# A compile-time scheduler that plans transfers on a shared server, tile turns apart from data, and the first rows in one buffer

## Chip, cores, metric

The kernel runs on one core of a Trainium2 chip. The metric is the device time of one execution in microseconds (us), the median of several runs. The engines are TensorE (PE in the profile, with its weight loader PEld), VectorE (DVE), ScalarE (ACT), GpSimd (POOL), and SyncE (SP), which issues all DMAs of this kernel.

## What is computed

Attention with normalised queries and keys (batch 8, 12 heads, 448 rows, head size 64), followed by two matrix products with `h * cos(h)` between them, all in float32:

```python
def rmsnorm(x, g):
    rms = np.sqrt(np.mean(x * x, axis=-1, keepdims=True) + 1e-06)
    return x / rms * g
q_n, k_n = (rmsnorm(q, g_q), rmsnorm(k, g_k))
scores = 1.0 / np.sqrt(64) * np.matmul(q_n, k_n.transpose(0, 1, 3, 2))
attn = np.exp(scores - np.max(scores, axis=-1, keepdims=True))
attn = attn / (np.sum(attn, axis=-1, keepdims=True) + 1e-09)
x = np.matmul(attn, v).transpose(0, 2, 1, 3).reshape(3584, 768)
h = x @ w_in                      # 768 x 2048
out = (h * np.cos(h)) @ w_out     # 2048 x 768
```

## The kernel before

**The work.** Two heads make a pair; there are 48 pairs `u`, six for each of the 8 batches `b`. Pairs 0 to 5 (`plain`) run in full float32. From pair 6 on each operand is split into a high part and a rest (`hi`, `lo`; `khi`, `kl`; `qhi`, `ql`) in a shorter float format, and products are sums over the parts.

For each pair: `st_load` brings the rows of q and k as `sd`; `st_square` (ACT) and `st_reduce` (DVE) make their sums of squares `r`; `st_pow` (POOL) makes the reciprocal roots; `st_store` and `rk_load` carry those of k through DRAM (`rk_d`) and back, spread over the partitions as `rkb`; `k_norm` and `q_scale` (POOL) apply them; `m_place`, `d_place` and `e_place` are DMAs that lay out the split operands for the score products. For the first two pairs (`turned`, `u < NKT`) k is normalised in rows (`kn_load`, `kn_square`, `kn_reduce`, `kn_pow`, `kn_norm`), turned by TensorE (`kn_turn`) and copied out as `km` (`kn_copy`, which needs the weight vector that `g_load` and `g_fold` make).

Then come seven score tiles per pair (`score_plain` or `score`, PE), `rowmin` (DVE), `expo` (ACT), the turning of the seven results (`transp`, PE, into the two banks `PT`), their copies (`pt_copy`, or `pt_high` on ACT and `pt_low` on DVE), and the product with v (`av`, PE).

The first product of the second layer, `ffn1`, of batch `b` fills TensorE between the attention steps of the next batch; its result `h` goes to DRAM (`h_out` on ACT into one of two `he` buffers, then `h_store`). Weights arrive as 64-bit numbers and are decoded to float32 in five steps (`w_load`, `w_decode` for w_in; `v_fetch`, `v_decode` for w_out), four on DVE and one on ACT. The second layer's product is a Strassen scheme: sums of quarters of w_out (`v_sum`, `v_split`) go back to DRAM (`wo_d`).

After the attention a second stage begins (at about 952 us): `ffn1_block` for the last batch, 16 blocks on 8 PSUM banks, block `fc` in bank `fc % 8`; meanwhile `h` is loaded back (`gl_load`), `h * cos(h)` is made and split, and `w_place` loads the weights of the second product from `wo_d` into slots that the w_in weights leave one by one. The rest is `ffn2`, in products P1 to P7, three banks each.

**The order.** Every step is handed to a class `Plan` with an engine, a cost in us, a due time, the keys it reads and writes, and, for a DMA, a time `land` from issue to data. `Plan.order()` then runs a list schedule at compile time: each engine takes, of the steps that can run, the one with the earliest due time. What comes out is only an order: each engine's instructions stand in its queue in this order, and the hardware's semaphores do the waiting. So a step that waits holds up all that stand behind it on its engine. `RING` says how many buffers a tile has; a tile's first user depends on all users of the tile that had the buffer before.

Of the kernel before, what the change touches and what calls it, by code (L numbers as in the profile page):

```python
# [10 lines left out]
F32 = mybir.dt.float32  # L11
# [12 lines left out]
class Plan:  # L24
# [3 lines left out]

    SIGNAL = {"PE": 0.25, "ACT": 0.19, "DVE": 0.16, "POOL": 0.15, "SP": 0.16}
    LEAD = 0.3

# [9 lines left out]
    def add(self, eng, cost, due, fn, *args, r=(), w=(), land=0.0, start=0.0, lead=None):  # L43
# [17 lines left out]
        self.parts.append((eng, cost, due, fn, args, deps, land))  # L61
# [3 lines left out]
    def order(self):  # L65
        parts = self.parts
        for (name, inst), users in self.users.items():
# [6 lines left out]
        left = [len(p[5]) for p in parts]  # L74
        ready = list(self.start)
        for n, p in enumerate(parts):
            for d in p[5]:
                after[d].append(n)
# [6 lines left out]
        seq = []  # L85
        self.busy = dict.fromkeys(free, 0.0)
        while True:
# [17 lines left out]
            cost, fn, args, land = (parts[n][i] for i in (1, 3, 4, 6))  # L105
            end = free[e] = t + cost
            self.busy[e] += cost
            seq.append((t, n, fn, args))
            for m in after[n]:
# [13 lines left out]
def tile_attention_moe(  # L123
# [163 lines left out]
    for t in qlow:  # L287
        nc.vector.tensor_scalar(
            t[64:128], ident[64:128, 0:1].broadcast_to([64, 384]), 0.0, 0.0, op0=ALU.mult, op1=ALU.add
        )  # L290
# [8 lines left out]

    def st_load(u):  # L300
        n = st_cols(u)
        nc.sync.dma_start(tl(u, "sd", [128, 14, D], F32)[:, :n], sd_in[u, :, :n])

    def st_square(u):
        sdf = pair[u]["sd"][:, : st_cols(u)].rearrange("p t d -> p (t d)")
        nc.scalar.activation(sdf, sdf, AF.Square)

    def st_reduce(u):
        n = st_cols(u)
        nc.vector.tensor_reduce(tl(u, "r", [128, 14], F32)[:, :n], pair[u].pop("sd")[:, :n], axis=AX.X, op=ALU.add)  # L310
# [393 lines left out]
    ISS, LAND = 0.45, 5.0  # L704
# [11 lines left out]
    add(SP, ISS, 0.0, g_load, w=[("g", 0)], land=LAND)  # L716
    add(DVE, 0.16, 10.0, g_fold, r=[("g", 0)], w=[("gsc", 0)])

    def weights(fc):
# [3 lines left out]
        add(SP, ISS, d - 30.0, w_load, fc, w=[w if f64 else f], land=8.0, start=begin)  # L723
# [11 lines left out]
    def weights2(c):  # L735
# [4 lines left out]
        for k in range(4):  # L740
            st, f, e = ("wf", NFC + 4 * c + k), qk[k], d + 0.1 * span * k
            if f64:
                add(SP, ISS, e - 20.0, v_fetch, c, k, w=[st], land=LAND, start=e - 30.0)
# [3 lines left out]
            else:  # L747
                add(SP, ISS, e - 20.0, v_fetch, c, k, w=[f], land=LAND, start=e - 30.0)
# [6 lines left out]
        for n, (name, src, _) in enumerate(SPLITS):  # L755
# [10 lines left out]
            add(SP, ISS, e + 5.0, v_store, c, p, r=[o], land=LAND)  # L766

    def prepare(u):
        D0 = base(u)
        sd, r, kd, khi, qd, qhi = ([(n, u)] for n in ("sd", "r", "kd", "khi", "qd", "qhi"))  # L770
        turned, plain = u < NKT, u < NP
        if turned:
            kn, rn, kb = [("qd" if u == 0 else "ql", u)], [("rn", u)], [("pt", 0, n) for n in ((0,) if u == 0 else (1, 2))]
            add(SP, ISS, D0 - 60, kn_load, u, w=kn, land=3.5)
# [6 lines left out]
        else:  # L781
            add(SP, ISS, D0 - 36, k_load, u, w=kd, land=LAND)
        add(SP, ISS, D0 - 45, st_load, u, w=sd, land=4.0 if turned else 6.5)
        add(SP, ISS, D0 - 44 if turned else D0 - 30, q_load, u, w=[("qp", u)] if plain else qd, land=3.5 if turned else LAND)
# [3 lines left out]
        if not turned:  # L788
            add(SP, ISS, D0 - 30, st_store, u, r=r, w=[("rkd", u)], land=LAND)
            add(SP, 2 * ISS, D0 - 26, rk_load, u, r=[("rkd", u)], w=[("rkb", u)], land=6.5)  # L790
# [313 lines left out]
```

## Time and profile before

| | |
|---|---|
| median of 3 runs | 1425.78 us (1423.07 to 1426.09) |
| profiled execution | 1433.95 us, of which the span from first to last instruction is 1432.0 us |
| mean granted TensorE clock | 0.993 |
| busy: PE, PEld | 1386.1 us (97%), 1196.7 us (84%) |
| busy: DVE, ACT, POOL | 1078.4 us (75%), 916.6 us (64%), 654.3 us (46%) |
| DMA | 301.88 MB, mean 211 GB/s |
| chain that ended last | PE 73%, DVE 13%, DMA 5%, ACT 3% |

The prediction's rows come from one profiled execution, and its times count from the span's start. A line L469 is line 469 of the kernel before. In a group or a timeline row, `S<-S,r` names the tile written and the tiles read; square brackets give the idle time of the engine before the instruction and what ended it.

### The profile page before, as it was taken

The page shows a single profiled execution, that of the slowest core. Times are in us where ns is not written, and L with a number is a line of the kernel's source. Part 1 is how long each engine was busy: PE and PEld are TensorE (multiplying, and loading weights), DVE is VectorE, ACT ScalarE, POOL GpSimd, SP SyncE. Part 2 cuts the span into 40 slices and gives each one's busy share as a digit, 9 for nine tenths or more (in the row PEclk, how much of TensorE's full clock was granted, in tenths as well). Part 3 has the DMA queues.
Part 4 walks back from the last instruction along what each step waited for, and adds up shares of the span by engine and source line. Part 5 has one row for each costly group of instructions (what it writes and reads, how often), then busy time and mean ns, then how long its engine had stood idle before and what let it go on. Part 6 is the DMA issues. An engine that isn't in the chain of part 4 may idle for free.

```text
span 1432.0 us, 22475 instructions
## 1 busy us (share of the span) xinstructions
PE 1386.1 (97%) x7118; PEld 1196.7 (84%) x7118; DVE 1078.4 (75%) x1864; ACT 916.6 (64%) x1868; POOL 654.3 (46%) x634
## 2 busy tenths in 40 slices
PE   5999999999999999999998999999999999999999
PEld 2346888889888888889897999989999999999998
DVE  6796999787878787786968665527669979879843
ACT  4676787777776866777776776646447457356331
POOL 5579988866866766686685674120000000000000
PEclk8999999999999999999999999999999999999999
DMA  6588767787778686867868765259768568468434
GB/s 217 174 241 244 207 166 212 219 243 230 232 221 243 204 249 202 241 197 227 241 203 249 203 204 143 73 173 341 235 197 296 162 212 298 144 222 289 125 108 146
DMA packets 169478, 301.88 MB, mean 211 GB/s; under 512 B 28512, under 2 KB 123568, under 8 KB 169360
## 3 DMA queue, kind: packets, MB, share of 16 engines
q1 hardware_dynamic: 169360, 300.45, 68.8%
q8 instruction: 56, 0.92, 0.3%
q14 instruction: 62, 0.51, 0.1%
HBM read 193.59 MB, written 62.73 MB: 179 GB/s over the span
## 4 chain that ended last, share of the span: by engine, by line
PE 73%; DVE 13%; DMA 5%; ACT 3%; issue 2%; SPq 1%; POOL 1%; POOLq 0%; DVEq 0%; ACTq 0%
PE y L683 10%; PE y L681 10%; PE y L682 10%; PE PT L510 7%; PE ph L614 6%; PE ph L615 6%; PE ph L616 6%; PE O L546 6%; PE S L465 6%; DVE S L469 3%; DVE lo L529 2%; PE y L615 1%; PE y L616 1%; PE y L614 1%; DMA rawo<-w_out 1%
## 5 line engine op out<-in xcount | busy, mean ns | idle before, releaser
L469 DVE TENSOR_SCALAR_CACHE_REDUCE S<-S,r 128x448 f32<-128x448 f32 x336 | 225.2, 685 | 71.5 <-PE S L465 65.4
L614 PE MATMUL ph<-xs,wi 128*128 128x448 f32 x672 | 256.5, 382 | 4.8 <-ACT he L626 4.7
L477 ACT ACTIVATE P<-S,sm 128x448 f32<-128x448 f32 x336 | 213.1, 636 | 70.8 <-DVE S L469 66.8
L681 PE MATMUL y<-g,wo 128*128 128x448 f32 x672 | 247.3, 368 | 0.0
L682 PE MATMUL y<-g,wo 128*128 128x448 f32 x672 | 247.3, 368 | 0.0
L683 PE MATMUL y<-g,wo 128*128 128x448 f32 x672 | 247.3, 368 | 0.0
L615 PE MATMUL ph<-xs,wi 128*128 128x448 f32 x672 | 246.2, 366 | 0.0
L616 PE MATMUL ph<-xs,wi 128*128 128x448 f32 x672 | 245.8, 366 | 0.0
L661 ACT CAST g<-gq 128x896 fp32r<-128x896 f32 x112 | 105.6, 943 | 184.1 <-PE y L683 161.7
L522 ACT CAST hi<-PT 128x512 fp32r<-128x512 f32 (+1 forms) x336 | 167.3, 533 | 70.5 <-PE PT L510 65.6
L510 PEld LDWEIGHTS PT<-ident,P 128*128 128x128 f32 (+1 forms) x1344 | 158.7, 134 | 49.3 <-issue 25.9
L529 DVE TENSOR_TENSOR lo<-PT,hi 128x512 fp32r<-128x512 f32 x252 | 149.8, 615 | 63.2 <-ACT hi L522 55.5
L510 PE MATMUL PT<-ident,P 128*128 128x128 f32 (+1 forms) x1344 | 195.7, 276 | 1.3 <-ACT P L477 1.3
L659 DVE TENSOR_TENSOR g<-gq,g 128x896 fp32r<-128x896 f32 x112 | 122.2, 1091 | 89.5 <-ACT g L661 89.0
L614 PEld LDWEIGHTS ph<-xs,wi 128*128 128x128 f32 x672 | 126.7, 189 | 17.5 <-ACT he L626 8.1
L683 PEld LDWEIGHTS y<-g,wo 128*128 128x128 f32 x672 | 126.1, 188 | 12.9
L682 PEld LDWEIGHTS y<-g,wo 128*128 128x128 f32 x672 | 126.1, 188 | 12.7
L681 PEld LDWEIGHTS y<-g,wo 128*128 128x128 f32 x672 | 126.1, 188 | 12.6
L616 PEld LDWEIGHTS ph<-xs,wi 128*128 128x128 f32 x672 | 126.5, 188 | 11.3
L615 PEld LDWEIGHTS ph<-xs,wi 128*128 128x128 f32 x672 | 126.9, 189 | 9.0
L316 POOL TENSOR_TENSOR r<-r,nhalf 128x14 f32<-128x14 f32 (+1 forms) x48 | 124.1, 2585 | 4.0
L546 PE MATMUL O<-hi,vs 128*128 128x448 f32 x336 | 121.3, 377 | 4.3 <-ACT hi L522 3.0
(102 smaller groups left out, 2602.9 us busy)
## 6 DMA issues: line engine op xcount, KB each, us to landing
wo<-wo_d SPq DMA_DIRECT2D x152, 384.0 KB
h_d<-he SPq DMA_DIRECT2D x128, 224.0 KB
gq<-h_d SPq DMA_DIRECT2D x64, 448.0 KB
wo_d<-ao SPq DMA_DIRECT2D x56, 384.0 KB
sd<-sd SPq DMA_DIRECT2D x46, 448.0 KB
D<-qhi SPq DMA_DIRECT2D x168, 96.0 KB
raw<-w_in SPq DMA_DIRECT2D x16, 768.0 KB
rawo<-w_out SPq DMA_DIRECT2D x32, 384.0 KB
```

The lines of the kernel that those rows point to most:

```text
L469: nc.vector.tensor_scalar(d["S", t][:, :S], d["S", t][:, :S], d["r"][:, t : t + 1], None, op0=ALU.mult, op1=ALU.min, accum_out=d["sm"][:, ...
L477: nc.scalar.activation(tl(u, f"P{t}", [128, S], F32, "P"), d.pop(("S", t))[:, :S], AF.Exp, bias=sm[:, 1, t : t + 1], scale=-1.0, accum_out ...
L510: nc.tensor.transpose(pt[part][:n, i * 128 : i * 128 + 128], src, ident)
L522: nc.scalar.copy(hi[:n], pt[part][:n, : WIDE[part]])
L529: nc.vector.tensor_tensor(lo, src, hi.bitcast(F32), ALU.subtract)
L546: nc.tensor.matmul(O, st, d[what, kc][:, HEADS[hh]], start=(kc + n == 0), stop=(kc == 3))
L614: nc.tensor.matmul(ph[:, :S], whi, x2[:, 0, :], start=(cc == 0), stop=False)
L615: nc.tensor.matmul(ph[:, :S], whi, x2[:, 1, :], start=False, stop=False)
L616: nc.tensor.matmul(ph[:, :S], wlo, x2[:, 0, :], start=False, stop=(cc == NCC - 1))
L681: nc.tensor.matmul(y, whi, hi[:, e], start=first and e == 0, stop=False, **more)
L682: nc.tensor.matmul(y, whi, lo[:, e], start=False, stop=False, **more)
L683: nc.tensor.matmul(y, wlo, hi[:, e], start=False, stop=last and e == NG - 1, **more)
```

## The change

No computation is added or taken away, and the cost and due time of every compute step stay. What differs:

1. **Transfers in the plan.** A DMA step now gives its size (`kb`) instead of a landing time. The plan keeps one clock `moved` for all transfers, which advances by size over 270 KB per us; a transfer is done at the later of its issue plus a flight by kind (5 to 7 us; 2.4 us for issues in the first 12 us) and `moved` plus 1.2 us.
2. **Tile turns apart from data.** Two dependencies that only keep tiles in their turn (the first user of one instance behind the first user of the one before; every user behind its tile's first user) no longer carry the landing and signal times, only the order.
3. **First rows.** The rows of pairs 0 and 1 share one `sd` buffer, half each, so that the second load needs no release.
4. **Early loads.** `k_load`, `st_load`, `q_load`, `v_plain` and `v_load` get start times tied to their pair; the three clears of the `E` tiles become steps of the plan (due 24 us) instead of standing at the head of DVE's queue.

Since every transfer's time is another in the plan, the order changes along the whole kernel, on all engines but TensorE in the second stage, whose order is the same.

The diff, cut to its core (the other lines replace `land=` by `kb=` with the transfer's size):

```diff
+    RATE = 270.0
+    FLIGHT = {
+        "st_load": 7.0, "m_place": 6.5, "d_place": 6.5, "e_place": 6.5, "v_load": 5.5, "v_fetch": 7.0, "w_load": 7.0,
+        "v_store": 6.0, "rk_load": 6.0, "rs_load": 6.0,
+    }
+    FLY = 5.0
...
         for (name, inst), users in self.users.items():
             parts[users[0]][5].update(self.users.get((name, inst - self.rings[name]), ()))
-            parts[users[0]][5].update(self.users.get((name, inst - 1), ())[:1])
             parts[users[0]][5].discard(users[0])
+            behind[users[0]].update(self.users.get((name, inst - 1), ())[:1])
             for n in users[1:]:
-                parts[n][5].add(users[0])
+                behind[n].add(users[0])
...
-            end = free[e] = t + cost
+            end = free[e] = done = t + cost
+            if kb:
+                moved = max(moved, end) + kb / self.RATE
+                fly = self.FLIGHT.get(fn.__name__, self.FLY) if t > 12.0 else 2.4
+                done = max(end + fly, moved + 1.2)
...
-                same = parts[m][0] == e and not land
-                gap = 0.0 if same else land + self.SIGNAL[e] + self.lead[m]
-                ready[m] = max(ready[m], end + gap)
+                if not full:
+                    ready[m] = max(ready[m], end)
+                elif parts[m][0] == e and not kb:
+                    ready[m] = max(ready[m], end)
+                else:
+                    ready[m] = max(ready[m], done + self.SIGNAL[e] + self.lead[m])
...
+    def sd_tile(u):
+        return pair[0]["sd"][:, 7 * u : 7 * u + 7] if u < NKT else pair[u]["sd"]
...
+        sd = [("sd", max(u, NKT - 1), u)]
...
-        add(SP, ISS, D0 - 45, st_load, u, w=sd, land=4.0 if turned else 6.5)
+        add(SP, ISS, D0 - 45, st_load, u, w=sd, kb=224.0 if turned else 448.0, start=0.0 if u < NP else D0 - 60)
...
+    for i in range(RING["E"]):
+        add(DVE, 0.31, 24.0 + i, e_clear, i, w=[("E0", i)], start=20.0)
```

What it moves, at three places. First, the head of SP's queue. Rows name the source line, the operation, the tile written and read, its shape, and how often the row repeats. Before, from the second `kn` on (`sd_113` and `sd_143` are the rows of pairs 0 and 1, `raw` a weight of w_in):

```order
L322 DMA kn_111<-kn 112x512
L302 DMA sd_113<-sd 128x448
L380 DMA q_98<-qT 128x512 x2
L181 DMA gs<-gg 128x2
L413 DMA vs_118<-v 128x512
L361 DMA kd_120<-kT 128x448
L380 DMA q_98<-qT 128x512 x4
L380 DMA qd_130<-qT 128x512
L410 DMA vd_135<-v 128x256
L199 DMA raw_139<-w_in 128x1536
L199 DMA raw_141<-w_in 128x1536
L302 DMA sd_143<-sd 128x448
```

After (`sd_110` holds the rows of both pairs):

```order
L324 DMA sd_110<-sd 128x448
L401 DMA q_98<-qT 128x512
L324 DMA sd_110<-sd 128x448
L401 DMA q_98<-qT 128x512
L198 DMA gs<-gg 128x2
L382 DMA kd_120<-kT 128x448
L216 DMA raw_123<-w_in 128x1536
L216 DMA raw_133<-w_in 128x1536
L434 DMA vs_143<-v 128x512
L324 DMA sd_148<-sd 128x896
L216 DMA raw_160<-w_in 128x1536
L401 DMA q_98<-qT 128x512
```

The rows of pair 1 moved from behind two `raw` loads to the place after the first q, and four of the later q loads moved back.

Second, ACT where the first pair in split form, pair 6, has its results turned (at about 120 us before). `hi_0` from the two `PT` banks is its first split tile, `khi` belongs to pair 8, and `sd` 128x896 is the square of a later pair. Before:

```order
L522 CAST hi_0_1124<-PT_105 128x512
L477 ACTIVATE P_1129,sm_923<-S_6_1105,sm_923 128x448
L485 ACTIVATE sm_923<-sm_923 128x7
L477 ACTIVATE P_1141,sm_1119<-S_3_1120,sm_1119 128x448
L369 CAST khi_1151<-kd_994 128x448
L306 ACTIVATE sd_1072<-sd_1072 128x896
L522 CAST hi_0_1124<-PT_106 128x384
L522 CAST hi_1_1173<-PT_105 128x512
```

The same place after:

```order
L543 CAST hi_0_1120<-PT_102 128x512
L543 CAST hi_0_1120<-PT_103 128x384
L390 CAST khi_1136<-kd_968 128x448
L408 CAST qhi_1143<-qd_995 128x512
L498 ACTIVATE P_1159,sm_1122<-S_3_1123,sm_1122 128x448
L498 ACTIVATE P_1170,sm_1122<-S_0_1131,sm_1122 128x448
L498 ACTIVATE P_1183,sm_1122<-S_4_1138,sm_1122 128x448
L543 CAST hi_1_1193<-PT_102 128x512
L543 CAST hi_1_1193<-PT_103 128x384
L328 ACTIVATE sd_1075<-sd_1075 128x896
```

Both halves of `hi_0` now follow each other, with `khi` and the square behind them. On DVE at the same place, `lo_0` is the rest of that tile and `TENSOR_REDUCE` the reduction of a later pair. Before:

```order
L469 TENSOR_SCALAR S_3_1120,sm_1119<-S_3_1120,r_713 128x448
L529 TENSOR_TENSOR lo_0_1139<-PT_105,hi_0_1124 128x512
L487 RECIPROCAL sm_923<-sm_923 128x7
L469 TENSOR_SCALAR S_0_1126,sm_1119<-S_0_1126,r_713 128x448
L310 TENSOR_REDUCE r_1171<-sd_1072 128x14
L529 TENSOR_TENSOR lo_0_1139<-PT_106,hi_0_1124 128x384
```

The same place after:

```order
L550 TENSOR_TENSOR lo_0_1129<-PT_102,hi_0_1120 128x512
L550 TENSOR_TENSOR lo_0_1129<-PT_103,hi_0_1120 128x384
L490 TENSOR_SCALAR S_3_1123,sm_1122<-S_3_1123,r_700 128x448
L490 TENSOR_SCALAR S_0_1131,sm_1122<-S_0_1131,r_700 128x448
L490 TENSOR_SCALAR S_4_1138,sm_1122<-S_4_1138,r_700 128x448
```

Both halves of `lo_0` follow each other, and the reduction stands further back.

Third, SP at the end of the last `ffn1` blocks in the second stage. `wo` rows are `w_place`, `h_d<-he_8` is the store of block 8. Before:

```order
L629 DMA h_d<-he_13_11934 128x448
L669 DMA wo_11871<-wo_d 128x768
L669 DMA wo_11962<-wo_d 128x768
L629 DMA h_d<-he_14_11964 128x448
L669 DMA wo_11905<-wo_d 128x768
L669 DMA wo_11970<-wo_d 128x768
L629 DMA h_d<-he_15_11968 128x448
```

The same place after:

```order
L650 DMA h_d<-he_7_11925 128x448
L690 DMA wo_11896<-wo_d 128x768
L690 DMA wo_11948<-wo_d 128x768
L650 DMA h_d<-he_8_11950 128x448
L690 DMA wo_11922<-wo_d 128x768
L650 DMA h_d<-he_9_11954 128x448
L690 DMA wo_11948<-wo_d 128x768
```

The two loads into the last slot (the tile `wo_11970` before and `wo_11948` after) begin ahead of the store of block 15 before, and ahead of that of block 8 after.

More of the change, by code (lines that the diff above doesn't have):

```diff
@@ L41, in __init__, with add @@
         self.users = {}
-    def add(self, eng, cost, due, fn, *args, r=(), w=(), land=0.0, start=0.0, lead=None):
+    def add(self, eng, cost, due, fn, *args, r=(), w=(), kb=0.0, start=0.0, lead=None):
         n = len(self.parts)
@@ L60, in add @@
         deps.discard(n)
-        self.parts.append((eng, cost, due, fn, args, deps, land))
+        self.parts.append((eng, cost, due, fn, args, deps, kb))
         self.start.append(start)
@@ L714, in ffn_due @@
         return base(NP * (b + 1) - 1) + SPLIT + i * (NP * PER / 48.0)
-    add(SP, ISS, 0.0, g_load, w=[("g", 0)], land=LAND)
+    add(SP, ISS, 0.0, g_load, w=[("g", 0)], kb=1.0)
     add(DVE, 0.16, 10.0, g_fold, r=[("g", 0)], w=[("gsc", 0)])
@@ L722, in weights @@
         begin = 4.0 + 3.0 * fc if fc < 3 else 24.0 + 7.0 * fc
-        add(SP, ISS, d - 30.0, w_load, fc, w=[w if f64 else f], land=8.0, start=begin)
+        add(SP, ISS, d - 30.0, w_load, fc, w=[w if f64 else f], kb=768.0 if f64 else 384.0, start=begin)
         if f64:
@@ L742, in weights2 @@
             if f64:
-                add(SP, ISS, e - 20.0, v_fetch, c, k, w=[st], land=LAND, start=e - 30.0)
+                add(SP, ISS, e - 20.0, v_fetch, c, k, w=[st], kb=384.0, start=e - 30.0)
                 for step, eng, cost in ((0, DVE, 0.5), (1, DVE, 0.65), (2, DVE, 0.6), (3, ACT, 0.45), (4, DVE, 0.55)):
@@ L747, in weights2 @@
             else:
-                add(SP, ISS, e - 20.0, v_fetch, c, k, w=[f], land=LAND, start=e - 30.0)
+                add(SP, ISS, e - 20.0, v_fetch, c, k, w=[f], kb=192.0, start=e - 30.0)
         sums = (
@@ L765, in weights2 @@
             add(POOL, 1.0, e + 2.0, v_split, c, p, src, True, r=[f], w=[o])
-            add(SP, ISS, e + 5.0, v_store, c, p, r=[o], land=LAND)
+            add(SP, ISS, e + 5.0, v_store, c, p, r=[o], kb=384.0)
     def prepare(u):
@@ L773, in prepare @@
             kn, rn, kb = [("qd" if u == 0 else "ql", u)], [("rn", u)], [("pt", 0, n) for n in ((0,) if u == 0 else (1, 2))]
[L774 removed]
+            add(SP, ISS, D0 - 60, kn_load, u, w=kn, kb=224.0)
             add(ACT, 0.62, D0 - 50, kn_square, u, r=kn, w=kb)
@@ L788, in prepare @@
         if not turned:
-            add(SP, ISS, D0 - 30, st_store, u, r=r, w=[("rkd", u)], land=LAND)
-            add(SP, 2 * ISS, D0 - 26, rk_load, u, r=[("rkd", u)], w=[("rkb", u)], land=6.5)
+            add(SP, ISS, D0 - 30, st_store, u, r=r, w=[("rkd", u)], kb=4.0)
+            add(SP, 2 * ISS, D0 - 26, rk_load, u, r=[("rkd", u)], w=[("rkb", u)], kb=224.0)
             if plain:
@@ L799, in prepare @@
                 add(POOL, 0.8, D0 - 16, q_scale, u, r=[("gsc", 0)], w=[("qp", u)])
-            add(SP, ISS, D0 - 12, v_plain, u, w=[("vs", u)], land=LAND)
+            add(SP, ISS, D0 - 12, v_plain, u, w=[("vs", u)], kb=256.0, start=D0 - 6)
             return
@@ L891, in attend @@
         D2 = D1 + 4 * step + 1
-        add(SP, 2 * ISS, D1 + 9, rs_load, u, r=[("rsd", u)], w=[("rs", u)], land=LAND)
+        add(SP, 2 * ISS, D1 + 9, rs_load, u, r=[("rsd", u)], w=[("rs", u)], kb=224.0)
         for hh in range(2):
@@ L976, in place_weights @@
         r = [] if first else [("w1", slot)]
-        add(SP, ISS, d, w_place, i, PRODUCT[name], c, r=r, w=w, land=8.0)
+        add(SP, ISS, d, w_place, i, PRODUCT[name], c, r=r, w=w, kb=384.0)
     for t in range(B // 2):
```

62 lines of the change are left out of this document (35 added, 27 removed).

## The prediction

> **What bounds the kernel now.** I read the page first, then the busy time by stage, then who waits for whom, then the timeline at the places where TensorE stands. By stage (us, busy us of each engine with the count of its instructions, granted TensorE clock, DMA share, GB/s):
>
> ```profile
> 0.00:20.00 20.00, 5.28 (x16) 2.51 (x16) 7.12 (x16) 4.51 (x7) 9.37 (x16) 0.98 0.85 288
> 20.00:120.00 100.00, 97.77 (x371) 40.20 (x372) 85.71 (x177) 72.61 (x167) 70.14 (x58) 0.94 0.66 199
> 120.00:140.00 20.00, 16.52 (x77) 13.94 (x76) 11.12 (x26) 12.05 (x28) 18.68 (x19) 0.83 0.96 260
> 140.00:952.00 812.00, 790.70 (x4362) 709.21 (x4360) 621.73 (x1284) 585.77 (x1387) 552.81 (x541) 1.00 0.71 205
> 952.00:1432.00 480.00, 475.84 (x2299) 430.88 (x2297) 352.71 (x364) 241.63 (x283) 3.26 (x3) 1.00 0.66 218
> ```
>
> From 952 us on TensorE has 475.84 of 480 us busy, and the rest is the tail after its last product: no order of the other engines can make that stage shorter, only longer. From 140 to 952 it has 790.70 of 812 busy. So the kernel is bound by TensorE's own work, and an order can win only what TensorE still loses: about 14.7 us of the first 20, 2.2 us to 120, 3.5 us in the 20 us after that (with the clock at 0.83), and the waits in the long middle. Those are read best on the weight loader, since a matmul that starts late counts as busy; from 140 to 952 us (us in total, times, longest):
>
> ```profile
> PEld O L546 <- DVE lo L529: 16.3, 28, 2.3
> PEld ph L614 <- ACT he L626: 8.1, 11, 2.1
> PEld O L546 <- DVE hi L531: 4.0, 8, 1.3
> PEld S L465 <- DMA h_d<-he: 3.7, 2, 2.2
> ...
> PEld S L465 <- DMA sd<-sd: 1.6, 1, 1.6
> ...
> PEld S L465 <- DMA E<-ql: 0.6, 1, 0.6
> ```
>
> The four smaller groups left out add 4.9 us, so the loader waits 39.2 us there. Some 28.4 us of it is for VectorE and ScalarE results (`lo` and `hi`, the split transposes, and `he`), and 5.9 us is put down to a DMA. VectorE is late because its queue is in order and the three decode steps of w_out stand in it.
>
> **The start.** The timeline (start us, duration us, engine, line, operation, idle before):
>
> ```profile
> 6.35 0.58 ACT L306 ACTIVATE sd<-sd 128x448 f32<-128x448 f32 x1 [1.15 <-DMA sd<-sd]
> 6.96 0.62 DVE L310 TENSOR_REDUCE r<-sd 128x7 f32<-128x448 f32 x1 [1.86 <-ACT sd L306]
> 7.61 0.93 DVE L288 TENSOR_SCALAR E<-ident 64x384 fp32r<-64x384 f32 x3
> ...
> 8.57 0.69 DVE L339 TENSOR_TENSOR kn<-kn,rn 112x512 f32<-112x512 f32 x1
> ...
> 10.36 1.63 POOL L334 TENSOR_TENSOR rn<-rn,nhalf 112x8 f32<-112x8 f32 x1
> ...
> 10.43 0.63 ACT L347 ACTIVATE km<-PT,gs 128x448 f32<-128x448 f32 x1 [3.50 <-PE PT L344]
> ...
> 12.02 1.87 DVE L339 TENSOR_TENSOR kn<-kn,rn 112x512 f32<-112x512 f32 x1 [1.98 <-POOL rn L334]
> 12.27 0.37 SPq L302 DMA_DIRECT2D sd<-sd  x1
> ...
> 13.82 0.68 DVE L469 TENSOR_SCALAR_CACHE_REDUCE S<-S,r 128x448 f32<-128x448 f32 x1
> ...
> 19.18 0.58 ACT L306 ACTIVATE sd<-sd 128x448 f32<-128x448 f32 x1 [8.12 <-DMA sd<-sd]
> 19.66 0.62 ACT L477 ACTIVATE P<-S,sm 128x448 f32<-128x448 f32 x1
> ...
> 20.43 6.58 PE L447 MATMUL S<-km,q 64*128 64x448 f32 x10 [5.01 <-ACT P L477]
> ```
>
> This is one chain. The rows of pair 1 need the one buffer of `sd` that pair 0 has, so their load is issued only at 12.27, after pair 0's have been reduced, and behind two weight loads of 768 KB. ScalarE has their square (19.18) ahead of the first `expo` in its queue, and so it idles 8.12 us, frees no score bank, and TensorE stands 5.01 us until 20.43.
>
> The change moves this load to the fifth place of the queue, two places behind pair 0's `sd`. The third load was squared at 6.35; the fifth has 480 KB more ahead of its end, 1.7 us at the 288 GB/s of this window, so it is there by about 8 to 9 us, before ScalarE or VectorE comes to it. VectorE's three clears of `E` (0.93 us at 7.61) move away from in front of `kn` (8.57), so that `kn_norm 0` starts about 0.95 us sooner; the gain shrinks to 0.5 us or nothing, since `g_fold` now stands behind two more reductions of 0.6 to 0.7 us and `km` (10.43) needs it. Then it goes by durations: `kn_pow 1` can begin when the POOL has done `st_pow 0` (about 9.6) and takes the 2.0 us it took before (from 10.07, its long step at 10.36); `kn_norm 1` at about 11.7, 0.69 us if it goes like `kn` at 8.57 (the 1.87 us at 12.02 lay beside POOL's `q_scale`, which now comes later); one `w_decode` step, 0.56 us as in the same group later; the first `rowmin`, 0.68 us plus the read of its accumulator, to about 13.8; the first `expo` to about 14.5, against 19.66 plus 0.62. TensorE gets its bank at about 14.5 instead of 20.43: 5.9 us. What takes from it: the clears (0.93 us) now lie between 20 and 40 us, where VectorE is busy 17.80 of 20 us, and `st_square 2` and a decode step (0.94 and 0.90 us) stand ahead of three of the `expo`, though they came soon after them before. On the other side `q_high 6` (0.62 us) leaves that stretch. I take **-5.5 us**. The ends are -6.5, where `km` gains as well and the clears are hidden, and -2, where all of it is paid and `kn_norm 1` is slow again (5.9 less 0.93, 1.84 and 1.18).
>
> The new order puts both 768 KB weights ahead of `vs 0` and `sd 2`. The row to weigh is 12.27: the load behind two such weights took until just before 19.18, about 6.8 us. The second `sd` load, issued after `st_reduce 1` at about 10, would land at about 16.9 by that row, and ScalarE comes to its square at about 16.4, so at worst half a microsecond is lost; most likely nothing, as the weights are 5 us old by then. This is inside the ends above. The Trainium skill says the same from the other side ("DMA: Bandwidth & Descriptors", Queues, rings and completion order): each DMA engine consumes its ring in order, so a small load behind large ones waits. By that rule the sum would be 0.5 us smaller, by the young age of the weights not.
>
> **The change of stage, 120 to 140 us.**
>
> ```profile
> 123.78 0.56 ACT L369 CAST khi<-kd 128x448 fp32r<-128x448 f32 x1 [1.28 <-POOL r L316]
> ...
> 124.25 0.95 ACT L306 ACTIVATE sd<-sd 128x896 f32<-128x896 f32 x1
> ...
> 125.10 0.95 ACT L522 CAST hi<-PT 128x384 fp32r<-128x384 f32 x2
> 125.23 1.09 DVE L310 TENSOR_REDUCE r<-sd 128x14 f32<-128x896 f32 x1 [2.22 <-DMA rs<-rs_d]
> ...
> 125.62 0.47 PE L546 MATMUL O<-hi,vs 128*128 128x448 f32 x1 [1.96 <-ACT hi L522]
> ```
>
> ScalarE takes `khi` of pair 8 (which waits for POOL) and the square of pair 11 before the second half of `hi` of pair 6; VectorE takes the reduction of pair 11 before `lo` of pair 6, and waits 2.22 us for it. TensorE stands 1.96 us for `hi` and then for `lo`. In the new order both halves of `hi 6` stand ahead of `khi`, both halves of `lo 6` follow each other, and the reduction of pair 10 comes a dozen rows behind them. After the stops the clock fell:
>
> ```profile
> 134.22 0.57 PE L615 MATMUL ph<-xs,wi 128*128 128x448 f32 x1
> 134.59 0.57 PE L616 MATMUL ph<-xs,wi 128*128 128x448 f32 x1
> ...
> 135.52 0.36 PE L616 MATMUL ph<-xs,wi 128*128 128x448 f32 x1
> 135.72 0.37 PE L546 MATMUL O<-hi,vs 128*128 128x448 f32 x1
> ```
>
> Start to start is 0.37 us at 134.22 and 0.20 at 135.52; the matmuls between 130.1 and 135.0, about 13, lost 0.17 us each, 2.2 us. With the 3.48 us idle that is 5.7 us. I take **-4 us**, since decode steps of weight 8 now stand ahead of `lo 6` of the second block and a load can still be late at a DMA share of 0.96. Ends: -5.7 (all gone), +2 (as long a wait at another place).
>
> **The middle, 140 to 952 us.** The costs of the compute steps are unchanged in the table of the scheduler; what changes is what it believes of transfers, and that a tile's turn no longer counts as data. From the chain (start, us, what):
>
> ```profile
> 95.95 5.67 DMA rk_d<-r
> ...
> 195.75 2.19 DMA rk_d<-r
> ...
> 436.80 5.55 DMA rawo<-w_out
> ...
> 755.09 6.33 DMA M<-kl
> ```
>
> Flights of 5.55 and 6.33 us stand here where the plan had 5.0 for each; the new table has 6.5 and 7.0, and a shared rate. So the waits put down to DMAs (5.9 us) should mostly go. The larger group, for VectorE, comes from decode steps that run longer than planned, which the change leaves; they fall elsewhere but do not vanish. I take **-4 us**, two thirds of the DMA group. Nothing in the trace of before shows how the other 33 us fall in the new order, so the ends are wide: -13 (a third of 39.2) and +10 (a quarter more).
>
> **The second stage's entry, 952 to 1015 us.** The order of TensorE is the same. SP's is not: there are two `he` buffers, so an `h_out` waits for the store of two before, and the new SP queue has the stores of the last block late. Store 8 stands behind the load into weight slot 15, which waits until TensorE has done the last `ffn1_block` with that slot. Before:
>
> ```profile
> 1011.64 0.37 PE L681 MATMUL y<-g,wo 128*128 128x448 f32 x1
> ...
> 1011.72 0.32 SPq L629 DMA_DIRECT2D h_d<-he  x1
> ...
> 1012.88 0.37 PE L681 MATMUL y<-g,wo 128*128 128x448 f32 x1
> ...
> 1014.45 0.55 ACT L626 ACTIVATE he<-y 128x448 f32<-128x448 f32 x1 [1.85 <-DMA h_d<-he]
> ```
>
> The last block ends at 1011.64, where the first `ffn2` product starts. Its third column group, at 1012.88, writes the bank of `h_out 10`, which now needs store 8. Store 8 can be issued after that load, with two issues of some 0.32 us (1011.72) and the hand-over from TensorE by about 1012.6, and from an issue ending at 1012.04 to the `he` it freed (1014.45) it took 2.4 us. So `h_out 10` runs from about 1015.0 to 1015.6, and TensorE, due at 1012.88, starts at 1015.7: **+2.8 us**, in a stage that had no wait. It is hidden by nothing: all products behind it shift. Ends: 0 (if `h_out` and its store ran far ahead, which the order of SP excludes unless the row with slot 15 is freed early), and +5.0, if the clock falls as it did at 130 us (2.2 us).
>
> Here a rule of the Trainium skill weighs in ("TensorE: Matmul & The Clock Gate", HAM oscillation): idle gaps up to about 3.4 us do not throttle the array. By it this stop of 2.8 us costs 2.8. The trace disagrees in part: at 123 to 130 us several stops, none above 2.0 us, were followed by 5 us at half rate, so the upper end stays.
>
> Other edits: `g_fold`, the plain `v`, `q` and `k` loads with start times and the later `q` loads have their consumers tens of steps behind them, so they cost nothing as long as the queue moves; SP is then the cover. The last stage's other moves lie beside a TensorE that is 0.99 busy and for which the other engines wait.
>
> **Sum.** -5.5 - 4 - 4 + 2.8 = -10.7 us. The profiled execution took 1433.95 us (span 1432.0), the median of the runs 1425.78, so it was 8 us slow; the change is subtracted from the median: 1415.1, forecast **1415**. For this kernel 0.2% is 2.85 us, about what its runs (1423.07 to 1426.09) can tell from nothing.
>
> **Rivals.**
> - *Deeper.* A plan whose transfers are true also places the decode steps truly, and half of the 28.4 us of waits for `lo`, `hi` and `he` go: 14 us where I have 0. For it: late loads hold up VectorE's and ScalarE's in-order queues, and some of those waits begin with one. Against: the chain in front of them is mostly decode and reduction. 1415 - 14 = 1401 at full size, 1404 at three quarters. Chance 0.17 (1400 to 1409).
> - *Given back.* The start wins 5.5 us, but the middle pays: the decode waits are as many and a fifth longer (+6 us of 28.4), and the entry stop stands. -5.5 - 4 + 6 + 2.8 = -0.7: 1425. For it: the long costs are untouched. Chance 0.21 (1421 to 1428).
> - *Late norms, slower.* The new order starts the chain square, power, store, `rkb`, `k_norm` of each pair later: 9 steps of SP lie between the store of `r` and the load that reads it, on average, where 30 did. At about 975 steps in 950 us that is 8.7 us against flights of 2.19 to 5.67 us in the rows above. It holds; but where a flight exceeds 8.7 us, SP itself stops and every load behind is late. If half of the 42 pairs lose 1 us so, +21 us: 1436. It decides from 8.7 us of flight on, or from 0.3 us lost in each pair (then it eats the 10.7). Chance 0.10 (1428 to 1440).
> - That the new order would not reach the start is excluded: the load stands fifth in the queue.
>
> **How the numbers follow.** The forecast's own range is 1409 to 1421, chance 0.52. With the three rivals the range that leaves out two in ten is 1403 to 1424. Faster by over 0.2% (below 1422.9): 0.52 + 0.17 + 0.08 of the given-back case = 0.77. Within 0.2%: 0.11 of that case and 0.02 of the late norms = 0.13. Slower: 0.02 and 0.08 = 0.10.
>
> **What would show it.** The square of pair 1 before 10 us, the first `expo` at about 14 us, no TensorE gap of 5 us near 15; the window 120:140 with over 18.5 us of TensorE busy and a clock near 1; fewer waits for DMAs in the middle; and a single gap of 2 to 4 us on the first `y` products of `ffn2`, released by `he`, with SP waiting for TensorE ahead of it. I am wrong if the loader's waits for `lo`, `hi` and `he` change by more than 10 us, if SP waits long for `rk_d`, or if the entry stop drops the clock.

## The result, and the profile after

The changed kernel takes **1414.1 us** (median of 6 runs, 1411.4 to 1419.1), the kernel before on the same chip 1425.3 us (1423.1 to 1426.1): the ratio is **0.993, 95% interval 0.991 to 0.995**, faster by 11.2 us. The forecast was 1415. The profiled execution after took 1414.5 us (span 1412.7), so it is like the median; the one before took 1433.95, since in its second stage TensorE went at a slower pace at the same clock (rows in the last section), as it did in some of the later runs. So the attention and the second stage are compared apart: the attention ends where TensorE's first `y` product starts (950.77 us before, 932.77 after), which lies ahead of the slower pace.

Busy time by stage after, in the columns of the same view before (us; busy us and count of PE, PEld, DVE, ACT, POOL; granted clock, DMA share, GB/s):

```profile
0.00:20.00 20.00, 9.71 (x25) 4.09 (x26) 11.32 (x26) 10.23 (x21) 9.36 (x16) 1.00 0.71 251
20.00:120.00 100.00, 96.01 (x395) 44.42 (x394) 85.73 (x177) 71.16 (x169) 78.54 (x66) 0.97 0.73 219
120.00:140.00 20.00, 18.07 (x94) 15.68 (x93) 18.65 (x37) 14.86 (x35) 16.15 (x15) 0.91 0.96 273
140.00:934.00 794.00, 780.68 (x4311) 704.00 (x4310) 603.75 (x1263) 579.26 (x1367) 548.24 (x537) 1.00 0.73 208
934.00:1412.70 478.70, 469.91 (x2299) 433.26 (x2297) 350.60 (x364) 242.16 (x283) 3.27 (x3) 0.99 0.66 218
```

The attention ends 18.0 us earlier. From 20 to 120 us TensorE does 395 products where it did 371, and from 120 to 140 us 94 for 77, but the clock there is 0.91, not 1. The last stage takes 478.7 us with 469.9 busy, where all 480 but the tail were busy before. Whom TensorE's weight loader (PEld) waits for, from 140 us to the end of the attention (in all, times, longest), 26.4 us in total where it was 39.2:

```profile
PEld O L567 <- DVE lo L550: 8.6, 18, 1.1
PEld O L567 <- DVE hi L552: 6.5, 5, 3.8
PEld ph L635 <- ACT he L647: 5.2, 11, 1.1
PEld O L567 <- issue: 2.6, 1, 2.6
PEld S L486 <- ACT P L498: 1.7, 4, 0.6
PEld PT L531 <- ACT P L498: 1.6, 4, 0.7
PEld ph L636 <- POOL xs L621: 0.2, 1, 0.2
```

No row names a DMA any more. The head (start, duration, idle before and what ended it), ScalarE and TensorE:

```profile
7.67 0.58 ACT L328 ACTIVATE sd<-sd 128x448 f32<-128x448 f32 x1 [0.67 <-DMA sd<-sd]
...
13.78 0.63 ACT L498 ACTIVATE P<-S,sm 128x448 f32<-128x448 f32 x1 [3.46 <-DVE S L490]
...
14.60 0.75 PE L468 MATMUL S<-km,q 64*128 64x448 f32 x1
...
31.29 0.93 ACT L233 ACTIVATE raw<-raw 128x768 f32<-128x768 f32 x1 [2.14 <-DVE wf L231]
...
33.34 0.57 ACT L576 COPY hi<-PT 64x512 f32<-64x512 f32 x1
...
33.96 0.96 PE L584 MATMUL O<-hi,vs 64*64 64x448 f32 x2 [1.88 <-ACT hi L576]
```

Pair 1's square runs at 7.67 us, the first `expo` at 13.78 (19.66 before), and TensorE gets the score bank it waits for at 14.60 (20.43 before). At 31 us a decode step of a weight holds ScalarE for 2.14 us, `hi` of pair 0 stands behind it, and TensorE waits 1.88 us. Below, the place of a pair is the start of its last product with v, its last `O` product: that of pair 0 moves from 42.7 to 36.3 us, of pair 1 from 58.8 to 54.2, of pair 5 from 118.7 to 113.7. The change of stage has stops still, at other places:

```profile
122.71 0.47 PE L567 MATMUL O<-lo,vs 128*128 128x448 f32 x1 [1.82 <-DVE lo L550]
...
154.37 0.44 PE L567 MATMUL O<-hi,vs 128*128 128x448 f32 x1 [2.21 <-DVE xf L607]
...
155.66 0.74 PE L567 MATMUL O<-lo,vs 128*128 128x448 f32 x1 [0.85 <-DVE lo L550]
```

At 122.71 VectorE is late with `lo` as before, and at 154 with `xf`. By pair 10 (213.5 us before) the lead is 7.5 us, by the end 18.0. Last, the entry of the second stage: TensorE, then ScalarE, then SP.

```profile
992.55 0.36 PE L702 MATMUL y<-g,wo 128*128 128x448 f32 x1
...
992.96 0.36 PE L704 MATMUL y<-g,wo 128*128 128x448 f32 x1
996.32 0.47 PE L702 MATMUL y<-g,wo 128*128 128x448 f32 x1 [2.99 <-ACT he L647]
...
998.80 0.74 PE L702 MATMUL y<-g,wo 128*128 128x448 f32 x1 [1.62 <-ACT he L647]
999.34 0.57 PE L703 MATMUL y<-g,wo 128*128 128x448 f32 x1
...
1004.85 0.37 PE L703 MATMUL y<-g,wo 128*128 128x448 f32 x1
...
991.17 0.55 ACT L647 ACTIVATE he<-y 128x448 f32<-128x448 f32 x1 [4.63 <-DMA h_d<-he]
995.72 0.54 ACT L647 ACTIVATE he<-y 128x448 f32<-128x448 f32 x1 [4.00 <-DMA h_d<-he]
998.21 0.54 ACT L647 ACTIVATE he<-y 128x448 f32<-128x448 f32 x1 [1.94 <-DMA h_d<-he]
...
986.76 3.13 SPq L690 DMA_DIRECT2D wo<-wo_d  x3
989.99 0.38 SPq L650 DMA_DIRECT2D h_d<-he  x1
990.41 2.65 SPq L690 DMA_DIRECT2D wo<-wo_d  x2
993.16 0.38 SPq L650 DMA_DIRECT2D h_d<-he  x1
```

The stop is there, with `he` as its releaser and SP between `wo` loads and stores, but it is two stops, 2.99 and 1.62 us, they start at the second column group, and after the second one the products come 0.37 us apart instead of 0.20 until 1004.85. The first 50 products of `ffn2` take 18.0 us (992.55 to 1010.53); at the full pace they take 10.1. The scheduler's own clock says where the SP order is from: by it TensorE's work of the second stage ends at 475.1 us in the kernel before and at 494.8 in the changed one, since it books each 384 KB weight with 1.4 us of a shared server and so has the stores of `he` late (that of block 7 at 30.3 us before, at 65.3 after).

### The profile page after: what moved, and what is told of

Its sections match the earlier page's. It is cut to its first block, busy times and chain, and to the rows that moved or that the text cites. A ratio compares the mean times of both kernels' runs of the same rounds, so it can differ in the third digit from the quotient of the medians.

```text
span 1412.7 us, 22533 instructions
## 1 busy us (share of the span) xinstructions
PE 1374.4 (97%) x7118; PEld 1201.4 (85%) x7118; DVE 1070.0 (76%) x1864; ACT 917.7 (65%) x1868; POOL 655.6 (46%) x634
## 4 chain that ended last, share of the span: by engine, by line
PE 76%; DVE 11%; DMA 4%; issue 3%; ACT 3%; POOL 2%; SPq 1%; POOLq 0%; ACTq 0%; DVEq 0%
PE y L702 10%; PE y L703 10%; PE y L704 10%; PE PT L531 7%; PE ph L635 7%; PE ph L636 7%; PE ph L637 7%; PE O L567 6%; PE S L486 6%; DVE S L490 3%; PE O L584 1%; DVE lo L550 1%; PE y L636 1%; PE y L637 1%; PE y L635 1%
## 5 line engine op out<-in xcount | busy, mean ns | idle before, releaser
L635 PE MATMUL ph<-xs,wi 128*128 128x448 f32 x672 | 257.2, 383 | 2.2 <-ACT he L647 2.0
L635 PEld LDWEIGHTS ph<-xs,wi 128*128 128x128 f32 x672 | 126.9, 189 | 15.5 <-ACT he L647 5.2
L637 PEld LDWEIGHTS ph<-xs,wi 128*128 128x128 f32 x672 | 126.8, 189 | 11.2
L703 PEld LDWEIGHTS y<-g,wo 128*128 128x128 f32 x672 | 127.0, 189 | 10.1
L704 PEld LDWEIGHTS y<-g,wo 128*128 128x128 f32 x672 | 126.9, 189 | 10.1
```

The costliest lines, as they stand in the source:

```text
L635: nc.tensor.matmul(ph[:, :S], whi, x2[:, 0, :], start=(cc == 0), stop=False)
L637: nc.tensor.matmul(ph[:, :S], wlo, x2[:, 0, :], start=False, stop=(cc == NCC - 1))
L703: nc.tensor.matmul(y, whi, lo[:, e], start=False, stop=False, **more)
L704: nc.tensor.matmul(y, wlo, hi[:, e], start=False, stop=last and e == NG - 1, **more)
```

## The experiments

All start from the changed kernel. Two switches give a plan back what it had: `landed` (landing times instead of flights and server) and `strict` (a tile's turn carries these times again), and the two plans (`RING` is that of the attention, `RING2` that of the second stage) can be set apart. The cuts show the lines that matter; `...` stands for lines left out:

```diff
 class Plan:
+    LAND0 = {"kn_load": 3.5, "st_load": 4.0, "q_load": 3.5}
+    LAND = {"w_load": 8.0, "w_place": 8.0, "st_load": 6.5, "rk_load": 6.5}
+    land = lambda s, f, a: s.LAND0[f] if f in s.LAND0 and a[0] < 2 else s.LAND.get(f, 5.0)
...
-                done = max(end + fly, moved + 1.2)
+                done = end + self.land(fn.__name__, args) if self.landed else max(end + fly, moved + 1.2)
...
-                if not full:
+                if not full and not self.strict:
```

**1. The old order in the second stage alone.**

```diff
     plan = Plan(RING2)
-    add = plan.add
+    add, plan.landed, plan.strict = plan.add, True, True
```

> The changed kernel, but the second stage is ordered by the transfers and turns of the plan before (landing times, no shared server); the attention keeps the new order. Theory (the entry alone): the two stops of TensorE at 993 and 997 us and the half rate behind them cost 7.7 us (the first 50 products of the last layer take 18.0 us instead of 10.3), and they come from the late stores of he in SP's new order. Then they vanish: about 1406.4 us (1405 to 1408.5), the first 50 products in 10.1 to 10.4 us, no wait for he over 1 us. Rival (handed on): the weights and h are late there in any order, since the stage now begins 18 us earlier behind the same loads, and another wait takes the place of the one for he: 1411 to 1414 us. Rival (the stop only): the half rate behind the stops is not theirs, and only the 4.9 us of idle time go, but not the rate: 1409 to 1410 us.

The profiled execution took 1406.5 us, which is the theory's number. The median of the six runs is 1416.8 (1406.5 to 1420.9), that of the kernel before beside them 1435.0 of 27, both, by their times, probably mostly at the slower pace; the ratio is 0.985 (0.982 to 0.988). TensorE and ScalarE at the entry, and then the window of the first products:

```profile
992.37 0.36 PE L702 MATMUL y<-g,wo 128*128 128x448 f32 x1
992.57 0.37 PE L703 MATMUL y<-g,wo 128*128 128x448 f32 x1
...
994.39 0.55 ACT L647 ACTIVATE he<-y 128x448 f32<-128x448 f32 x1 [0.84 <-DMA h_d<-he]
996.57 0.55 ACT L647 ACTIVATE he<-y 128x448 f32<-128x448 f32 x1 [1.63 <-DMA h_d<-he]
```

```profile
992.40:1005.00 12.60, 12.60 (x64) 11.68 (x63) 10.46 (x11) 4.96 (x7) 0.00 (x0) 1.00 0.94 330
```

The attention is the same to 0.2 us (932.59), no product waits, `he` is still made after stores (0.84 and 1.63 us) but nobody needs it, and DMA moves 330 GB/s there, where the plan's server gives it 270 KB per us, about 276. The first 50 products take 10.1 us. The entry costs the change **7.7 to 7.9 us** (18.0 less the 10.3 of the kernel before, or the 10.1 of this run): 4.6 us of stops, and the half rate is the rest.

**2. The old plan in both stages: the first rows, start times and late clears alone.**

```diff
     plan = Plan(RING)
-    add = plan.add
+    add, plan.landed, plan.strict = plan.add, True, True
...
     plan = Plan(RING2)
-    add = plan.add
+    add, plan.landed, plan.strict = plan.add, True, True
```

> The changed kernel with the plan before in both stages (landing times, turns as data): what is left of the change are the first rows in one buffer, the start times of the early loads and the clears of E as steps. Theory (terms stand apart): the start keeps its gain of about 5 us and nothing else is won or lost: 1420.3 us (1418 to 1422); first expo at about 14 us, TensorE's first score product at 14.5 to 16; the stops of the change of stage at 120 to 130 us as before (some 5 us), the loader's waits from 140 to the end of the attention about 39 us. Rival (chance): the order is so sensitive that any change of the plan's input moves the middle by several us either way: outside 1416 to 1424, between 1408 and 1432 us, with the loader's waits in the middle off by more than 6 us from 39.

Profiled 1418.7 us; the median of 12 runs is 1431.6, the ratio to before 0.996 (0.994 to 0.998). The start gains even more than in the change: the last product of pair 0 comes 8.5 us earlier than before, that of pair 2 7.3 us. Then all of it is gone: that of pair 3 comes 0.2 us later than before, of pair 9 6.8 us. The rows of that place, from POOL, ScalarE and TensorE:

```profile
72.92 3.17 POOL L337 TENSOR_TENSOR r<-r,nhalf 128x14 f32<-128x14 f32 x1
...
78.55 1.34 POOL L405 TENSOR_SCALAR qd<-qd,gs 128x512 f32<-128x512 f32 x1 [1.50 <-DMA qd<-qT]
79.85 1.82 POOL L387 TENSOR_TENSOR kd<-kd,rkb 128x448 f32<-128x448 f32 x1
...
81.70 0.56 ACT L390 CAST khi<-kd 128x448 fp32r<-128x448 f32 x1 [5.92 <-POOL kd L387]
82.18 0.63 ACT L498 ACTIVATE P<-S,sm 128x448 f32<-128x448 f32 x1
...
82.95 1.86 PE L468 MATMUL S<-km,q 64*128 64x448 f32 x2 [3.28 <-ACT P L498]
```

POOL waits for a load of q (1.50 us) behind a long `st_pow`, so `k_norm` is late; ScalarE has `khi` of that pair ahead of two `expo` and stands 5.92 us, frees no score bank, and TensorE stands 3.28 us and then runs at half rate. The attention still ends 6.4 us earlier than before, but the gain comes after pair 20. So this part is no separate term of 5 us: what the start wins lasts only if the order behind it holds. The profiled total fell near the theory (1420.3) by luck, for another reason than it gave. And the waits of the loader for DMA rows are gone here too (0.5 us left of 5.9), without the new plan.

**3 and 4. One half of the new plan at a time, in the attention.** The second stage keeps its new order.

```diff
     plan = Plan(RING)
-    add = plan.add
+    add, plan.landed, plan.strict = plan.add, True, False    # run 3: old landing times, turns without them
+    add, plan.landed, plan.strict = plan.add, False, True    # run 4: flights and server, turns with them
```

> The changed kernel, but the attention's plan has the landing times of before instead of flights by kind and a shared server; tile turns stay apart from data, and the second stage has its new order (with its stops). Theory A (true transfers make the gain of the middle): the 11 us of the middle and the 2 us of the change of stage are gone: 1425 to 1429 us, with waits for DMA rows of some 6 us on the loader again. Theory B (the turns make it): 1412 to 1416 us, as the change. Rival (chance): 1417 to 1424 us or under 1411, whichever of the two is taken away.

> The changed kernel, but in the attention's plan a tile's turn carries landing and signal times again, as before; flights by kind and the shared server stay, and the second stage has its new order (with its stops). Theory A (true transfers make the gain of the middle): 1412 to 1416 us, as the change, and no waits for DMA rows on the loader. Theory B (the turns make it): 1425 to 1429 us. Rival (chance): 1417 to 1424 us or under 1411, and together with the run before this one the two losses do not add up to 13 us.

Profiled 1427.7 and 1439.7 us, medians 1427.9 of 10 and 1433.9 of 12, ratios to before 0.995 (0.992 to 0.998) and 0.999 (0.997 to 1.001). TensorE in both went over to its slower pace in the second stage, so the attention's end decides: 938.6 and 949.7 us, against 932.6. (Run 3's 1427.7 lies in the range of theory A only by this pace.) Taking away the server loses 6 us, taking away the free turns 17: together 23, though both halves are worth 11.7 us (944.3 - 932.6). Neither theory holds, and the server without the free turns is worse than the old plan whole (949.7 against 944.3). The scheduler's own clock knew of the large loss: it ends the attention at 920.7 us in the change, at 939.4 in run 4 (and, by the old landing times, at 924.2 in run 3).

**5. The new plan alone,** with the rows, the start times and the clears of before; the second stage has the old plan, as in experiment 1.

```diff
-        return pair[0]["sd"][:, 7 * u : 7 * u + 7] if u < NKT else pair[u]["sd"]
+        return pair[u]["sd"][:, : st_cols(u)]
...
-        sd = [("sd", max(u, NKT - 1), u)]
+        sd = [("sd", u)]
...
-    add(DVE, 0.31, 24.0 + i, e_clear, i, w=[("E0", i)], start=20.0)
+    add(DVE, 0.31, -90.0 + i, e_clear, i, w=[("E0", i)])
```

(and the `start=` of `k_load`, `st_load`, `q_load`, `v_plain` and `v_load` left out)

> The first experiment's kernel (new plan in the attention, old plan in the second stage) without the first rows in one buffer, the start times of the early loads and the late clears of E: the plan alone. The measure is TensorE's first y product, the end of the attention: 950.8 us before, 932.6 in the first experiment, 944.3 with the rows and the old plan. Theory (the two parts stand apart): the plan wins 950.8 - 932.6 - 6.4 = 11.8 us by itself: 937 to 941 us, with the start's stop of 5 us before 20.4 us back. Rival (they need each other: either part's gain is given back at 75 to 200 us, where all transfers are busy, unless the other is there): 945 to 951 us.

The attention ends at 943.7 us (one execution, 1417.7 us in all), between the ranges of theory and rival: the plan alone wins 7.1 us, the rows, start times and clears alone 6.4, both 18.2.

**6, 7, 11, 12. A number without meaning.** Experiment 1's kernel with another `RATE`:

```diff
-    RATE = 270.0
+    RATE = 260.0     # 280.0, 240.0
```

> The first experiment's kernel with a planned rate of the transfers of 260 instead of 270 KB per us in the attention: a change of the plan with no meaning for the chip. Theory (the gain is the plan's): the first y product at 930.5 to 935.5 us, as at 270 (932.6). Rival (chance: the order is sensitive, and the 11 us of the middle are one draw): 936 to 949 us, or under 930.

> The first experiment's kernel with a planned rate of 280 instead of 270 KB per us in the attention, the second draw of the same kind. Theory (the gain is the plan's): the first y product at 930.5 to 935.5 us. Rival (chance): 936 to 949 us, or under 930; with the draws at 260 and 270 a spread of over 5 us.

The run at 260 tells nothing of the order: its clock was 0.754 from the first slice to the last, and it took 1676.9 us; it stands again below. At 280 the attention ends at 945.09 us, **12.5 us later than at 270**, for 4% of a number that no hardware reads. It is one execution, so what an order varies by itself has to be put beside it: the attention of the change ended at 932.77 and 932.59 us in its two profiles, and the six runs of experiment 1 lie within 14.5 us, 9.3 of which a change of pace can account for. The 1428.3 us at 280, at the slower pace, are 7.4 above the slowest of them. The pace has no part in the 12.5: from 140 us to the end of the attention, products that follow each other closely come 0.204 us apart in both. Differences of 5 us between single executions tell less. The rows of the first `y` product in the kernel before, the change, and at 280 (line L635 is L614 before):

```profile
950.77 0.37 PE L614 MATMUL y<-xs,wi 128*128 128x448 f32 x1
```

```profile
932.77 0.37 PE L635 MATMUL y<-xs,wi 128*128 128x448 f32 x1
```

```profile
945.09 0.37 PE L635 MATMUL y<-xs,wi 128*128 128x448 f32 x1
```

Until pair 0 all is as in the change (5.8 us ahead of before, 6.4 there); at pair 5 it is 3.4 us behind the kernel before, at pair 10 4.7, and from there to the end it wins 10.4 as the change does (10.5). So the order of 280 loses its 12 us between pair 0 and pair 10, from 37 to about 215 us, the stretch in which the 16 weights of w_in are decoded as well.

**8. Turns of the placing steps only,** from experiment 1's kernel.

```diff
-                after[d].append((n, False))
+                after[d].append((n, p[3].__name__ in self.NAMES))    # "m_place", "d_place", "e_place"
```

> The first experiment's kernel, but the steps that place the split operands of the scores (m_place, d_place, e_place) again wait in the plan for the landing of their tile's first user and of the turn before; all other turns stay order alone. In the plan before, the two halves of M of one head were so laid at least 6.5 us apart, and those of the next head behind them. Theory (it is these turns that cost the attention 17 us when all turns carry landing times, 949.7 against 932.6): the first y product at 943 to 950 us. Rival (it is the turns of the row and weight loads): 931 to 936 us. Rival (chance): 936 to 943 us, or under 930.

939.8 us: 7 of the 17 us, 5 of them by pair 10 (by the scheduler's own clock 935.1, 14 of its 19). It is the size of the differences that a changed rate makes, so it gives these steps no part of their own.

**9 to 12. Does the plan tell which order is good?** The scheduler's own clock ends the attention at 920.7 us for 270, 924.3 for 280. Of the rates from 240 to 330, in steps of 5, 320 ends earliest (914.7); it, 315, 260 and 240 were run, from experiment 1's kernel.

> The first experiment's kernel with a planned rate of 320 instead of 270 KB per us. Of the rates from 240 to 330 this is the one whose plan ends earliest by the scheduler's own clock (attention's last product at 914.7 us; 920.7 at 270, measured end of the attention 932.6; 924.3 at 280, measured 945.1). Theory (sensitive, but the plan's own end tells which order is good): the first y product at 924 to 931 us, and about 1400 us in all with TensorE at 203 ns per product, 1410 at 207. Rival (chance: the plan's own end tells nothing): anywhere from 932 to 949 us, as the other orders did.

> The first experiment's kernel with a planned rate of 315 KB per us (planned end of the attention 917.7 us). Theory (the plan's own end tells): the first y product at 927 to 934 us. Rival (chance): 935 to 949 us.

> The kernel with a planned rate of 260 KB per us once more (planned end of the attention 924.8 us), since its first run fell into a clock of 0.75 from the first microseconds on. Theory (the plan's own end tells): the first y product at 940 to 948 us. Rival (the gain is the plan's at any rate): 930.5 to 935.5 us. Rival (chance): either, or between.

> The first experiment's kernel with a planned rate of 240 KB per us (planned end of the attention 927.2 us, the latest of the rates from 240 to 330). Theory (the plan's own end tells): the first y product at 942 to 952 us. Rival (the gain is the plan's at any rate): 930.5 to 935.5 us. Rival (chance): 932 to 942 us, or before another rate whose plan ends earlier.

| rate, KB/us | end by the plan | first `y` product, measured | time (one execution, but for 320) |
|---|---|---|---|
| 320 | 914.7 | 926.5 | **1400.3** median of 6, ratio 0.982 (0.980 to 0.984) |
| 315 | 917.7 | 930.2 | 1404.1 |
| 270 | 920.7 | 932.6 | 1406.5 (median of 6: 1416.8, probably mostly at the slower pace) |
| 280 | 924.3 | 945.1 | 1428.3 (slower pace in the second stage) |
| 260 | 924.8 | 927.0 | 1401.0 |
| 240 | 927.2 | 939.5 | 1413.7 |

The three that end first by the plan come in its order, 12 us over it each. But 280 and 260, half a microsecond apart in the plan, are 18 us apart on the chip, so the theory fails for the others: the scheduler's clock told a difference of 19 us (run 4) but not one of 4. Six rates give 926.5 to 945.1, with a mean of 933.5; the change's 270 is an ordinary one of them. All six lie below the 950.8 of before, five below the 944.3 of the rows with the old plan. Rate 320 with the old second stage beats both kernels: 25.7 us less than before (1426.06, median of its 11 runs there). Its loader waits, 140 us to the end of the attention, 20.7 us in all:

```profile
PEld O L567 <- DVE lo L550: 6.0, 11, 1.5
PEld ph L635 <- ACT he L647: 5.3, 7, 1.4
PEld O L567 <- DVE hi L552: 4.1, 6, 1.3
PEld S L486 <- ACT P L498: 3.0, 3, 1.8
PEld S L486 <- DMA M<-kl: 1.5, 1, 1.5
PEld S L486 <- DMA E<-ql: 0.8, 1, 0.8
```

Two waits for DMA rows are back, 2.3 us, and it is the fastest all the same: `lo` and `he` are down to 11.3 us from 24.4 before.

## Why the prediction was right, and where it was not

The time was right (1415 for 1414.1), the sum was not: two of its four terms were wrong by more than 4 us, with opposite signs. By the ends of pairs 5, 10 and 47 and by the entry, the measured terms are about -5.0, -2.5, -10.5 and +7.7, together -10.3 against -10.7 forecast and -11.2 by the medians.

- **Start, -5.5: right in its steps, in its size in part by luck.** Each step came within a microsecond of its place (7.67 for 8 to 9, 13.78 for 14.5, 14.60 for 14.5). But the term left out the clock, though the row from 20 to 120 us showed 0.94. Before, half rate stood behind the stop of 5.01 us (clock 0.50 from 19.23 to 29.47 us); the change has full rate there, and the lead grows from 5.8 us to 8.7 at the twelfth product of pair 0 (30.66 for 39.38). Then the stop behind the decode step at 31 us, which was not foreseen either, and the half rate that follows it (0.50 from 35.35 to 42.17) take it back to 4.5 at the end of pair 1; at pair 5 it is 5.0. And experiment 2 shows that the term is not one by itself: with the old plan the same start wins 8.5 us and gives all of it back 40 us later.
- **Change of stage, -4: too much, -2.5** (by pair 10, which ends long after 140 us; by pair 6, at 139.6 us before, it is -2.1). Both halves of `hi` and `lo` did come together, but `lo` was late at 122.71 for 1.82 us and two more stops followed at 154. TensorE has 18.07 us busy at a clock of 0.91, where the prediction asked for over 18.5 and near 1.
- **Middle, -4: mis-sized, -10.5.** The step "the waits put down to DMAs should mostly go" came true (5.9 us to none), but not by the plan's flights alone: they also go, but for 0.5 us, with the old plan of experiment 2. The larger part came from what was said to "fall elsewhere but do not vanish": `lo`, `hi` and `he` together fell from 28.4 to 20.3 us. That was the rival *Deeper* (half of the 28.4 were to go), and its reason, transfers that are true in the plan, does not hold either: with five other rates in the same plan the stretch from pair 10 on wins between 3.4 and 16.8 us. It is one order out of many, and the step had only its wide ends (-13 and +10) to say so.
- **Entry, +2.8: mis-sized, +7.7.** The mechanism was right (two `he` buffers, stores behind `wo` loads that wait for TensorE). The step reckoned with one late store and one stop. In the trace each of the last stores stands about 3 us behind loads (986.76: three loads in 3.13 us), so `h_out` is late one group earlier and twice, and the half rate, named as what would make the prediction wrong, costs some 3 us more (clock 0.50 for 6.8 us; the prediction put such a spell at 2.2). Its upper end was 5.0.
- **The base was right.** The 8 us by which the profiled execution before was slow lie behind 955 us (below), and all but some 1.5 us of them outside the stretches of the terms, so subtracting from the median was the correct use.

So the number came out by luck: two misses of 6.5 and 4.9 us nearly cancel. What stays open: why one rate's order loses 12 us between 37 and 215 us and another's doesn't. The stops are spread over `hi`, `lo`, `expo` and decode steps, and no one run here takes the decode steps out.

## What to carry to other kernels

Where a planner writes in-order queues, the parts of a change to it don't add: try a number of it that means nothing (here 4% of a rate moved the attention by 12.5 us), and price a change of the planner as a draw with that spread before naming a cause for it. Then use it: a few orders by the same planner, run and compared, with the second stage set apart, gave 13.8 us more (1414.1 to 1400.3, some 7.8 of it from the old order of the second stage), where the change gave 11.2. Read each stage's queues apart, too; a model of transfers that suits a stage which waits for them can put stores behind loads in one that doesn't.

## What the runs showed of the hardware

**Two paces of TensorE at the same granted clock.** A stretch of the second stage before and after, no product waits in either:

```profile
1115.00:1165.00 50.00, 50.00 (x244) 45.41 (x243) 40.22 (x43) 19.05 (x23) 0.00 (x0) 1.00 0.44 129
```

```profile
1115.00:1165.00 50.00, 50.00 (x249) 46.33 (x248) 39.36 (x41) 23.45 (x29) 0.00 (x0) 1.00 0.59 183
```

The clock is 1.00 in both, yet before it does 244 products in 50 us and after 249. Start to start they are 0.2067 us apart, each, in one pace; in the other the distances go 0.207, 0.202, 0.203, 0.202, 0.199, mean 0.2026. In each case seen the pace is taken up where TensorE restarts after waits (before at 955 us; in run 3 after the stops at 999 to 1005 us) and lasts to the end: about 2280 products at 0.0041 us are 9.3 us; the profiled execution before was 8.7 us over the median of the six runs beside the change. The unprofiled times of the kernel before fall in two groups of about that distance (1423 to 1428 and 1432 to 1437 us, with five from 1439 to 1445), which fits, and no run here shows what chooses.

**Half rate goes by stretches of 3.41 us.** In the clock records of these profiles the granted clock changes only at steps of 3.41 us, and each spell at 0.50 lasts one to three steps. So what a stop does depends on where the steps cut it. Three such stretches, two after the change and one in experiment 1:

```profile
994.50:997.91 3.41, 0.87 (x3) 0.48 (x3) 0.00 (x0) 0.54 (x1) 0.00 (x0) 1.00 1.03 402
```

```profile
711.19:714.60 3.41, 1.54 (x8) 1.08 (x6) 3.38 (x3) 1.77 (x5) 3.41 (x3) 1.00 1.02 323
```

```profile
710.84:714.25 3.41, 0.54 (x3) 0.16 (x1) 3.35 (x4) 0.77 (x3) 3.41 (x3) 1.00 0.93 252
```

The first holds most of the two stops at the entry: TensorE is busy 0.87 of 3.41 us, and from 997.91 to 1004.73 the clock is 0.50. The second and third hold the same stop in the same order of the attention. After the change it is 3.37 us long (the row below), a step at 714.60 cuts it in two, TensorE is busy 1.54 us ahead of the step and 1.92 in the stretch behind it, and the products come 0.20 us apart at once. In experiment 1 it is 3.36 us long, 0.54 us are busy in one stretch, and the clock is 0.50 from 714.25 to 717.67.

```profile
716.10 0.47 PE L567 MATMUL O<-hi,vs 128*128 128x448 f32 x1 [3.37 <-DVE hi L552]
```

In the 13 profiles other than the one at 0.754, from 20 to 1395 us, each of the 16 stretches at full clock in which TensorE was busy 40% or less was followed by 0.50. Between 44 and 56% it was 10 of 21, above that 4 of 5149, all four before 85 us. The Trainium skill ("TensorE: Matmul & The Clock Gate", HAM oscillation) gives idle gaps over about 3.4 us as the limit. The trace does not agree: the stop of 2.21 us at 154 was enough (1.20 us busy from 151.40 to 154.81, then 0.50 until 161.64), and the one of 3.37 was not.

**A lower clock for a whole execution.** The first run at rate 260 had a granted clock of 0.754 on the mean and took 1676.9 us; the same kernel took 1401.0 at 0.999. No run here shows why.
